# The tail of a fused convolution and SiLU network: the last block's second half, output bank by output bank in another order

## The chip, the cores and the metric

The kernel runs on one core of one Trainium2 chip. The metric is device time in microseconds (us): the median of the runs shown, each of which is one execution of the whole program. The engines are named as in the profile: PE is the matrix engine (PEld its weight loads), DVE the vector engine, ACT the scalar engine, POOL the general-purpose engine, SP the engine that issues most transfers. A `q` behind a name (ACTq, SPq) means the engine's own instruction queue, which also issues its transfers.

## The reference

The reference is a lightweight convolution followed by a two-layer network with SiLU between the layers, without a bias. Cut to what matters:

```python
# x: (8, 4096, 192), weight: (8 heads, 7 taps), softmax over the taps
w   = softmax(weight, axis=-1)
y   = causal depthwise convolution of x, 7 taps, 24 channels per head
h   = y.reshape(32768, 192) @ w_in        # w_in: (192, 2048)
g   = h * sigmoid(h)
out = g @ w_out                           # w_out: (2048, 192)
```

Everything is in float32.

## The kernel before, in words

The 32768 tokens are cut into 32 blocks of 1024 tokens, and a block into two halves of 512 (`TB`). Block 0 is computed by plain matrix products. Blocks 1 to 31 use a fast (Strassen-like) scheme in both layers: fewer products of 2x2 blocks, paid for by sums and differences on DVE, ACT and POOL. The order of the work within a block is written out by hand in `PLAN` (lines 66 to 101): each slot between bars names the products of the first layer (`P..`, `E..`), the evictions and SiLUs (`s..`, `C..`, `g..`) and the differences of the second layer (`t.jk`). `pin` (line 103) holds an instruction behind the instruction that was written before it on the same engine, transfers that this engine issues among them. The transfers themselves are not pinned.

The second layer ("the second half" of a block) gathers its result in six accumulation banks, `accs[b][0..5]`, each of 128 partitions by 512 float32 columns. `out_slot(b, j, i, e)` (line 482) issues the products of bank `i` for one of 4 groups `j` of hidden units and one of two halves `e` of such a group: four products, each of which fills 32 partitions of the bank. Partitions 0 to 95 of banks 0 to 4 hold a product of their own; partitions 96 to 127 hold a third of a further product, whose pieces have to be brought to partitions 0 to 95 before they can be added. Bank 5 holds the last piece of one of these in 4 times 128 columns. So the pieces of banks 0, 1 and 2 make up `y`, those of banks 4, 3 and 5 make up `x_`. With `half` given, a slot covers 256 of the 512 columns (a "token half").

The four outputs of a block are quarters of 96 channels by 512 tokens, `c[0]` to `c[3]` (the fast scheme's C11, C21, C12, C22 in the order that the code uses: index modulo 2 is the token half of the block, index divided by 2 the channel half):

```
c[0] = acc0 + y
c[1] = acc0 + acc2 + acc1 + acc4
c[3] = acc0 + acc2 + acc4 + acc3
c[2] = acc0 + acc2 + acc3 + x_
```

Bank 0 reaches all four quarters, bank 2 three, banks 3 and 4 two, bank 1 one, and each set of pieces one.

In blocks 1 to 30 the second half of a block is overlapped with the convolution for the block after it. The last block (31) has nothing behind it. Its groups `j` = 0 and 1 go through `down` (line 520) as in the others, bank by bank within a group; then `finish` (line 651) issues the groups 2 and 3 in an order of its own. Within it `step(b, "t.jk")` makes the differences for group `j` (line 480, DVE, 128 x 1024; `t.j0`, `t.j1` lie in one tile, `t.j2`, `t.j3` in a second). Bank 0 and bank 1 need no differences, bank 2 needs `t.j1`, bank 4 needs `t.j0` and `t.j3`, bank 3 needs `t.j2` and `t.j3`, bank 5 needs `t.j3`. The tiles of the differences come from `tpool`, which has three buffers.

Before the change `finish` issues, for each of the two groups, banks 2, 4, 3 and 5; then bank 0 for both groups, then bank 1 for both groups, by token halves. Lines 688 to 701 read banks 2, 4, 3 and 5 while PE works on banks 0 and 1. Lines 710 to 715 add bank 0 to the quarters and store `c[3]` and `c[2]`. Lines 716 to 722 add bank 1 and store `c[1]` and `c[0]` by token halves; there POOL makes the sum `c[0] + y` (line 721).

`store` (line 673) transposes a quarter in blocks of 32 x 32 on DVE into `osb` and issues three transfers to memory, the first and third on SP, the second on ACT. All DVE and ACT instructions in `finish` are pinned, the POOL sum and the transfers are not. In the profile all pinned DVE instructions of `finish` carry line 111, the line of the helper.

Of the kernel before, what the change touches and what calls it, by code (L numbers as in the profile page):

```python
# [9 lines left out]
F32 = mybir.dt.float32  # L10
I32 = mybir.dt.int32
AF = mybir.ActivationFunctionType
ALU = mybir.AluOpType
# [4 lines left out]
def kernel(  # L18
# [24 lines left out]
    nc = tc.nc  # L43
# [6 lines left out]
    P = 128  # L50
# [4 lines left out]
    TB = 512  # L55
# [4 lines left out]
    NJ = NM // 2  # L60
    SQ = 32
    HD = D // 2
    NP = HD // SQ
# [6 lines left out]
    xpool = ctx.enter_context(tc.tile_pool(name="xp", bufs=1))  # L70
    tpool = ctx.enter_context(tc.tile_pool(name="tp", bufs=3))
# [31 lines left out]
    def pin(ins):  # L103
        return tc.keep_in_program_order(ins)
# [5 lines left out]
        def __getattr__(self, name):  # L110
            return lambda *args, **kw: pin(getattr(self.engine, name)(*args, **kw))  # L111

    vec = Pinned(nc.vector)

    def bank():
        return psum.tile([P, TB], F32, tag="ps", name="ps")
# [170 lines left out]
    for e in range(2):  # L287
        half = hot[R * e : R * e + R]
# [24 lines left out]
    for k in range(NK):  # L313
# [4 lines left out]
            op=ALU.mult,  # L318
# [96 lines left out]
    bk, us, sums, cmbs, accs = {}, {}, {}, {}, {}  # L415

    def product(b, m, name):
        d, t = dups[b], wins[b]
        e, r, s = m % 2, wr[m // 2], ws[m // 2]

        other, bn, w, v = {
            "P1": (0, "1", r[:, 0, 0, :], d[:, 0, 0, :]),
            "P6": (0, "1", r[:, 0, 1, :], t[:, 1, :]),
            "P7": (0, "1", r[:, 1, 0, :], t[:, 2, :]),
            "P4": (0, "1", r[:, 1, 1, :], t[:, 3, :]),
            "E21": (0, "1", r[:, 1, 2, :], d[:, 0, 2, :]),
            "P2": (1, "b", s[:, 0, 1, :], d[:, 0, 1, :]),
            "E11": (1, "b", s[:, 0, 2, :], d[:, 0, 2, :]),
            "P5": (1, "d", s[:, 1, 0, :], t[:, 0, :]),
            "E22": (1, "d", s[:, 1, 2, :], d[:, 1, 2, :]),  # L430
            "P3": (1, "d", s[:, 0, 0, :], d[:, 1, 1, :]),
            "E12": (1, "d", s[:, 1, 1, :], d[:, 1, 2, :]),
        }[name]
        half = e ^ other
        first = (b, m, bn) not in bk
        if first:
            bk[b, m, bn] = bank()
        pin(
            nc.tensor.matmul(  # L439
                bk[b, m, bn], rows(w, half), rows(v, half), start=first, stop=True,  # L440
                skip_group_check=True,
            )
        )
# [38 lines left out]
    def out_slot(b, j, i, e, half=None):  # L482

        g = [gs[b, j, a] for a in range(2)]
        w, x_ = wo[j], wx[j]
        if i not in accs.setdefault(b, {}):
            accs[b][i] = bank()

        def t(k):
            return sums[b, j][k // 2][:, k % 2, :].rearrange("p (e t) -> p e t", e=2)

        a_ = [[w[:, a, :, HD * u : HD * u + HD] for a in range(2)] for u in range(2)]
        forms = {
            1: lambda: (a_[0][0], g[0][:, 0]),
            2: lambda: (a_[0][1], g[1][:, 0]),
            3: lambda: (x_[:, 2], g[1][:, 1]),
            4: lambda: (a_[1][1], t(3)),
            5: lambda: (x_[:, 0], t(0)),  # L500
            6: lambda: (x_[:, 1], t(1)),
            7: lambda: (a_[1][0], t(2)),
        }
        own, other, c = ((1, 2, 0), (3, 2, 1), (6, 2, 2), (7, 4, 0), (5, 4, 1), (4, 4, 2))[i]
        for q in range(4):
            lhs, rhs = forms[own if q < NP else other]()
            k = c if i == 5 or q == NP else q
            to = slice(0, TB // 4) if i == 5 else slice(0, TB) if half is None else ts(half, TB // 2)
            pin(
                nc.tensor.matmul(  # L510
                    accs[b][i][SQ * q : SQ * q + SQ, to],
                    lhs[:, e, SQ * k : SQ * k + SQ],
                    rhs[:, e, ts(q, TB // 4) if i == 5 else to],
                    start=j == 0 and e == 0,
                    stop=j == NJ - 1 and e == 1,
                    skip_group_check=True,
                )
            )
# [72 lines left out]
    osbs = {}  # L591
# [21 lines left out]
    def step(b, token):  # L613

        if token[0] == "-":
            b, token = b - 1, token[1:]
        name, arg = token.split(".") if "." in token else ("", "")
        if b < 0 or b >= NB or not name or (b, token) in did:
            return
        did.add((b, token))  # L620
        digits = [int(c) for c in arg]
        if name[0] in "PE":
            product(b, digits[0], name)
        elif name[0] in "sCg":
            if b:
                sums_h(b, name, digits[0])
        elif name == "t":
            sum_g(b, *digits)
        elif name[0] in "Mzyx":
            merge(b, name)  # L630
        elif name == "o":
            turn_out(b, *digits)
        elif b + 1 < NB:
            {"i": turn_in, "v": conv, "w": win}[name](b + 1, *digits)
            if name == "v" and digits[1] == K - 1 and (b, "down") in did:
                spread(b + 1, digits[0])
                if digits[0] == NK - 1 and b + 2 < NB:
                    load(b + 2)
# [12 lines left out]
    def finish(b):  # L651


        late = (NJ - 2, NJ - 1)
        for j in late:
            for k in (0, 1, 3, 2):
                step(b, f"t.{j}{k}")
            for i in (2, 4, 3, 5):
                for e in range(2):
                    out_slot(b, j, i, e)  # L660
        acc, n = accs[b], HD
        cmb = xpool.tile([P, 4, TB], F32, tag="cmb", name="cmb")
        cmbs[b] = [cmb]
        c = [cmb[0:n, i, :] for i in range(4)]
        y, x_ = (upool.tile([P, TB], F32, tag="u", name="u") for _ in range(2))

        def part(t, k):
            return t[SQ * k : SQ * k + SQ, :]

        def add(out_, u, v):  # L670
            vec.tensor_tensor(out_, u, v, op=ALU.add)

        def store(i, cols, rows_=slice(0, n)):

            if b not in osbs:
                osbs[b] = tpool.tile([P, 4, TB // SQ, SQ], F32, tag="t", name="osb")
            osb = osbs[b][:, i, :, :].rearrange("p k c -> p (k c)")
            vec.transpose(osb[rows_, cols], cmb[rows_, i, cols])
            ks = slice(cols.start // SQ, cols.stop // SQ)
            for q in range(rows_.start // SQ, rows_.stop // SQ):  # L680
                ch = HD * (i // 2) + SQ * q
                (nc.sync, nc.scalar, nc.sync)[q % 3].dma_start(
                    out=out_v[2 * b + i % 2][:, ks, ch : ch + SQ],
                    in_=osbs[b][SQ * q : SQ * q + SQ, i, ks, :],
                )

        every = slice(0, TB)
        pin(nc.scalar.copy(c[1], acc[2][0:n, :]))
        pin(nc.scalar.copy(part(y, 2), acc[2][n:P, :]))
        pin(nc.scalar.copy(part(x_, 1), acc[4][n:P, :]))  # L690
        add(c[2], c[1], acc[3][0:n, :])
        pin(nc.scalar.copy(part(x_, 0), acc[3][n:P, :]))
        add(c[3], c[2], acc[4][0:n, :])
        add(c[1], c[1], acc[4][0:n, :])
        for q in range(4):
            pin(
                nc.scalar.copy(
                    part(x_, 2)[:, ts(q, TB // 4)], acc[5][SQ * q : SQ * q + SQ, 0 : TB // 4]
                )
            )  # L700
        add(c[2], c[2], x_[0:n, :])
        for j in late:
            for e in range(2):
                out_slot(b, j, 0, e)
        for half in range(2):
            for j in late:
                for e in range(2):
                    out_slot(b, j, 1, e, half)
            if half == 0:
                for k in (3, 2):  # L710
                    add(c[k], c[k], acc[0][0:n, :])
                    store(k, every)
                add(c[1], c[1], acc[0][0:n, :])
                pin(nc.scalar.copy(c[0], acc[0][0:n, :]))
                pin(nc.scalar.copy(part(y, 0), acc[0][n:P, :]))
        for half in range(2):
            cols = slice(half * TB // 2, (half + 1) * TB // 2)
            add(c[1][:, cols], c[1][:, cols], acc[1][0:n, cols])
            pin(nc.scalar.copy(part(y, 1)[:, cols], acc[1][n:P, cols]))
            store(1, cols)  # L720
            nc.gpsimd.tensor_tensor(c[0][:, cols], c[0][:, cols], y[0:n, cols], op=ALU.add)
            store(0, cols)


    for k in range(NK):
# [36 lines left out]
    for b in range(1, NB):  # L762
# [9 lines left out]
        slots = (None for j in range(NJ // 2 if last else NJ) for _ in down(b, j))  # L772
# [34 lines left out]
```

## Time and profile before

| | us |
|---|---|
| median of 4 runs | 2423.1 (2422.9 to 2423.46) |
| profiled execution, device time | 2422.9 |
| its span, first to last instruction | 2421.2 |
| PE busy | 2390.0 (99% of the span) |
| DVE busy | 2077.5 (86%) |
| ACT busy | 982.6 (41%) |
| POOL busy | 64.5 (3%) |
| first product of `finish` (group 2) | at 2393.76 |
| first product of bank 0 in `finish` | at 2404.94 |
| first product of bank 1 in `finish` | at 2408.37 |
| last product ends | at 2412.01 |
| last transpose starts | at 2416.50 |

Times "at" are counted from the start of the span. The device time is 1.7 us longer than the span, which is what lies around the instructions. A row of the timeline gives start, length, engine, line, operation, output and inputs with their shape, the number of instructions taken together, and in brackets how long the engine had been idle and what ended that idle time. Rows of transfers show when they were issued; the time to landing comes from the view of the transfers.

### The profile page before, as it was taken

What the parts mean: (1) busy time and instruction counts of PE and PEld (TensorE: products, weight loads), DVE (VectorE), ACT (ScalarE), POOL (GpSimd) and SP (SyncE); (2) the same over time, 40 slices, a digit from 0 to 9 for tenths busy, and PEclk for the clock granted to TensorE, in tenths of its full rate; (3) what the DMA queues carried; (4) which work ended last, traced back from release to release, by engine and by line L of the source; (5) the groups of instructions that cost most, each with busy time, mean ns of one, the idle gap of its engine ahead of it and who ended that gap; (6) DMA issues with size and microseconds to landing.
All of it is one profiled execution on the core that took longest, in us unless ns stands there. A gap on an engine that the chain in (4) does not pass through costs nothing.

```text
span 2421.2 us, 43109 instructions
## 1 busy us (share of the span) xinstructions
PE 2390.0 (99%) x17776; PEld 956.9 (40%) x17776; DVE 2077.5 (86%) x2831; ACT 982.6 (41%) x1847; POOL 64.5 (3%) x98
## 2 busy tenths in 40 slices
PE   6999999999999999999999999999999999999998
PEld 4444433334333344333444333443334433334433
DVE  8988888898888988888988889888889888898876
ACT  3134533345433355333454334543334533345432
POOL 3300000000000000000000000000000000000000
PEclk9999999999999999999999999999999999999999
DMA  7321222222222212222222222122222222222220
GB/s 152 73 52 32 45 44 54 41 43 40 37 54 49 43 33 39 50 53 40 41 37 43 53 45 46 34 36 53 53 41 39 36 45 54 43 40 41 36 40 14
DMA packets 454085, 111.65 MB, mean 46 GB/s; under 512 B 423936, under 2 KB 429056, under 8 KB 453888
## 3 DMA queue, kind: packets, MB, share of 16 engines
q1 hardware_dynamic: 450064, 106.89, 23.7%
q8 instruction: 139, 2.28, 0.4%
q0 software_dynamic: 480, 1.58, 0.3%
q10 hardware_dynamic: 3344, 0.42, 0.1%
q14 instruction: 58, 0.48, 0.1%
HBM read 31.49 MB, written 25.17 MB: 23 GB/s over the span
## 4 chain that ended last, share of the span: by engine, by line
PE 98%; DVE 1%; DMA 0%; SPq 0%; issue 0%; ACT 0%; ACTq 0%; POOLq 0%; POOL 0%; DVEq 0%
PE ps L439 49%; PE ps L510 46%; PE ps L538 2%; PE ps L403 2%; DVE nat L353 0%; DMA nat<-in_x_dram 0%; SPq L127 0%; DMA raw<-in_moe_w_in_dram 0%; DVE two L111 0%; DVE cmb L111 0%; DVE osb L111 0%; DVE xt L333 0%; DVE nat L350 0%; DVE mh L111 0%; ACT two L201 0%
## 5 line engine op out<-in xcount | busy, mean ns | idle before, releaser
L439 PE MATMUL ps<-dup,ws 64*128 64x512 f32 x2480 | 869.7, 589 | 0.0
L510 PE MATMUL ps<-g,wo 128*32 128x512 f32 x2984 | 662.2, 592 | 0.0
L463 DVE TENSOR_TENSOR g<-u,ps 128x512 f32<-128x512 f32 x744 | 485.2, 679 | 117.7 <-PE ps L439 88.9
L439 PE MATMUL ps<-win,wr 64*128 64x512 f32 x1488 | 568.8, 589 | 0.1
L510 PE MATMUL ps<-t,wo 128*32 128x512 f32 (+1 forms) x4464 | 500.7, 450 | 0.0
L460 ACT ACTIVATE g<-g 128x512 f32<-128x512 f32 x744 | 444.6, 631 | 99.4 <-DVE g L463 99.4
L439 PEld LDWEIGHTS ps<-dup,ws 64*128 64x128 f32 x2480 | 364.1, 187 | 289.0 <-issue 273.4
L510 PE MATMUL ps<-t,wx 128*32 128x512 f32 x2976 | 452.9, 592 | 0.0
L353 DVE SCALAR_TENSOR_TENSOR nat<-xt,taps,nat 128x512 f32<-128x512 f32 x576 | 431.9, 750 | 15.1
L439 PE MATMUL ps<-dup,wr 64*128 64x512 f32 x992 | 419.3, 596 | 0.0
L454 ACT COPY u<-ps 128x512 f32<-128x512 f32 x496 | 277.8, 588 | 228.4 <-PE ps L439 225.5
L577 ACT COPY cmb<-ps 96x512 f32<-96x512 f32 x30 | 17.4, 581 | 805.5 <-PE ps L510 805.5
L480 DVE TENSOR_TENSOR t<-g,t 128x1024 f32<-128x1024 f32 x248 | 303.4, 1223 | 19.1 <-PE ps L510 8.3
L480 DVE TENSOR_TENSOR t<-g 128x1024 f32<-128x1024 f32 x248 | 299.6, 1219 | 22.7 <-PE ps L510 22.7
L439 PEld LDWEIGHTS ps<-win,wr 64*128 64x128 f32 x1488 | 234.3, 187 | 173.7 <-issue 144.5
L510 PEld LDWEIGHTS ps<-t,wo 128*32 128x32 f32 x4464 | 178.3, 110 | 222.6 <-issue 204.9
L439 PE MATMUL ps<-win,ws 64*128 64x512 f32 x496 | 241.9, 589 | 0.0
L510 PE MATMUL ps<-g,wx 128*32 128x512 f32 (+1 forms) x1512 | 234.6, 585 | 0.0
L510 PEld LDWEIGHTS ps<-t,wx 128*32 128x32 f32 x2976 | 121.9, 110 | 277.6 <-issue 268.3
L589 DVE TENSOR_TENSOR cmb<-cmb,ps 96x512 f32<-96x512 f32 x150 | 102.3, 682 | 135.2 <-ACT u L574 133.1
L439 PEld LDWEIGHTS ps<-dup,wr 64*128 64x128 f32 x992 | 160.8, 187 | 126.8 <-issue 111.7
L510 PEld LDWEIGHTS ps<-g,wo 128*32 128x32 f32 x2984 | 169.4, 110 | 98.3 <-issue 98.3
(67 smaller groups left out, 1211.1 us busy)
## 6 DMA issues: line engine op xcount, KB each, us to landing
dup<-nat SPq DMA_DIRECT2D x384, 128.0 KB, 2.3
nat<-in_x_dram SPq DMA_DIRECT2D x382, 64.0 KB, 2.5
out_dram<-osb SPq DMA_DIRECT2D x376, 64.0 KB, 2.0
raw<-in_moe_w_in_dram SPq DMA_DIRECT2D x16, 192.0 KB, 4.9
raw<-in_moe_w_out_dram SPq DMA_DIRECT2D x8, 384.0 KB, 3.6
ws<-wr POOLq DMA_DIRECT2D x8, 192.0 KB, 4.4
xt<-xt SPq DMA_DIRECT2D x31, 4.5 KB, 1.9
tail<-xt SPq DMA_DIRECT2D x24, 4.5 KB, 1.9
```

Source lines behind the costliest of these rows:

```text
L353: nc.vector.scalar_tensor_tensor(out=dst, in0=src, scalar=tap, in1=dst, op0=ALU.mult, op1=ALU.add)
L403: nc.tensor.matmul(hs[a, n, e], rows(wr[j], e)[:, a, k, :], rows(d, e)[:, n, k, :], start=k == 0, stop=k == NK - 1,)
L439: nc.tensor.matmul(bk[b, m, bn], rows(w, half), rows(v, half), start=first, stop=True, skip_group_check=True,)
L454: pin(copy(u, bk[b, m, "1"]))
L460: pin(nc.scalar.activation(g, g, AF.Silu))
L463: pin(nc.vector.tensor_tensor(g, us.pop((b, m, i)), bk[b, m, bn], op=ALU.add))
L480: pin(nc.vector.tensor_tensor(t[i // 2][:, i % 2, :], u, v, op=ALU.subtract))
L510: nc.tensor.matmul(accs[b][i][SQ * q : SQ * q + SQ, to], lhs[:, e, SQ * k : SQ * k + SQ], rhs[:, e, ts(q, TB // 4) if i == 5 else to], sta ...
L538: nc.tensor.matmul(acc[k][R * n : R * n + R, :], wo[j][:, a, e, R * k : R * k + R], gs[b, j, a][:, n, e, :], start=j == 0 and a == 0 and e ...
L577: pin(nc.scalar.copy(c[0], acc[0][0:n, :]))
L589: pin(nc.vector.tensor_tensor(out_, u, v, op=ALU.add))
```

## The change

It rewrites the order of `finish`. All products, sums, transposes and transfers are still there, apart from what follows.

- The order of the banks is 0, 1, 2, 4 with both groups for each, then bank 3 for its first token half, bank 5, and bank 3 for its second token half. The differences `t.j0`, `t.j1` come first, `t.j3` ahead of bank 2, `t.j2` behind the first sum of `c[2]`.
- `c[0]` and `c[1]` are summed and stored whole; `c[3]` and `c[2]` are finished and stored by token halves at the end. Within the loop over halves, the sums and the store of a half stand between the products of bank 3 for this half and those for the next.
- The sum `c[0] + y` moves from POOL to DVE and is one instruction of 512 columns.
- The copies on ACT are pinned as before, through `act`. Five of them (`c[0]`, and the pieces of banks 0, 1, 2 and 4) cover 512 columns, those of bank 3 are by token halves.
- The second tile of differences for group 3 uses the buffer of `win`, and `osb` the buffer of `dup`, both of which the first layer has done with by then, in place of buffers of `tpool`.

```diff
-    vec = Pinned(nc.vector)
+    vec, act = Pinned(nc.vector), Pinned(nc.scalar)
...
-        for j in late:
-            for k in (0, 1, 3, 2):
-                step(b, f"t.{j}{k}")
-            for i in (2, 4, 3, 5):
-                for e in range(2):
-                    out_slot(b, j, i, e)
-        acc, n = accs[b], HD
+        sums[b, NJ - 1] = {1: xpool.tile([P, 2, 2 * TB], F32, tag="win", name="t")}
...
-                osbs[b] = tpool.tile([P, 4, TB // SQ, SQ], F32, tag="t", name="osb")
+                osbs[b] = xpool.tile([P, 4, TB // SQ, SQ], F32, tag="dup", name="osb")
...
-        pin(nc.scalar.copy(c[1], acc[2][0:n, :]))
-        pin(nc.scalar.copy(part(y, 2), acc[2][n:P, :]))
-        pin(nc.scalar.copy(part(x_, 1), acc[4][n:P, :]))
-        add(c[2], c[1], acc[3][0:n, :])
-        pin(nc.scalar.copy(part(x_, 0), acc[3][n:P, :]))
-        add(c[3], c[2], acc[4][0:n, :])
-        add(c[1], c[1], acc[4][0:n, :])
-        for q in range(4):
-            pin(
-                nc.scalar.copy(
-                    part(x_, 2)[:, ts(q, TB // 4)], acc[5][SQ * q : SQ * q + SQ, 0 : TB // 4]
-                )
-            )
-        add(c[2], c[2], x_[0:n, :])
-        for j in late:
-            for e in range(2):
-                out_slot(b, j, 0, e)
-        for half in range(2):
+        def slots(i, half=None):
             for j in late:
                 for e in range(2):
-                    out_slot(b, j, 1, e, half)
-            if half == 0:
-                for k in (3, 2):
-                    add(c[k], c[k], acc[0][0:n, :])
-                    store(k, every)
-                add(c[1], c[1], acc[0][0:n, :])
-                pin(nc.scalar.copy(c[0], acc[0][0:n, :]))
-                pin(nc.scalar.copy(part(y, 0), acc[0][n:P, :]))
+                    out_slot(b, j, i, e, half)
+
+        for j in late:
+            for k in (0, 1):
+                step(b, f"t.{j}{k}")
+        acc = accs[b]
+        slots(0)
+        act.copy(c[0], acc[0][0:n, :])
+        act.copy(part(y, 0), acc[0][n:P, :])
+        slots(1)
+        act.copy(part(y, 1), acc[1][n:P, :])
+        for j in late:
+            step(b, f"t.{j}3")
+        slots(2)
+        act.copy(part(y, 2), acc[2][n:P, :])
+
+        add(c[2], c[0], acc[2][0:n, :])
+        for j in late:
+            step(b, f"t.{j}2")
+        add(c[0], c[0], y[0:n, :])
+        store(0, every)
+        add(c[1], c[2], acc[1][0:n, :])
+        slots(4)
+        act.copy(part(x_, 1), acc[4][n:P, :])
+        add(c[1], c[1], acc[4][0:n, :])
+        store(1, every)
+        add(c[3], c[2], acc[4][0:n, :])
         for half in range(2):
             cols = slice(half * TB // 2, (half + 1) * TB // 2)
-            add(c[1][:, cols], c[1][:, cols], acc[1][0:n, cols])
-            pin(nc.scalar.copy(part(y, 1)[:, cols], acc[1][n:P, cols]))
-            store(1, cols)
-            nc.gpsimd.tensor_tensor(c[0][:, cols], c[0][:, cols], y[0:n, cols], op=ALU.add)
-            store(0, cols)
+            slots(3, half)
+            if half == 0:
+                slots(5)
+            add(c[3][:, cols], c[3][:, cols], acc[3][0:n, cols])
+            store(3, cols)
+            act.copy(part(x_, 0)[:, cols], acc[3][n:P, cols])
+            if half == 0:
+                for q in range(4):
+                    act.copy(
+                        part(x_, 2)[:, ts(q, TB // 4)], acc[5][SQ * q : SQ * q + SQ, 0 : TB // 4]
+                    )
+            add(c[2][:, cols], c[2][:, cols], acc[3][0:n, cols])
+            add(c[2][:, cols], c[2][:, cols], x_[0:n, cols])
+            store(2, cols)
```

The rest of the program, blocks 0 to 30 and the first half of block 31 among it, is the same.

More of the change, by code (lines that the diff above doesn't have):

```diff
@@ L654, in finish @@
         late = (NJ - 2, NJ - 1)
-        for j in late:
-            for k in (0, 1, 3, 2):
-                step(b, f"t.{j}{k}")
-            for i in (2, 4, 3, 5):
-                for e in range(2):
-                    out_slot(b, j, i, e)
-        acc, n = accs[b], HD
+        sums[b, NJ - 1] = {1: xpool.tile([P, 2, 2 * TB], F32, tag="win", name="t")}
         cmb = xpool.tile([P, 4, TB], F32, tag="cmb", name="cmb")
         cmbs[b] = [cmb]
+        n = HD
         c = [cmb[0:n, i, :] for i in range(4)]
         y, x_ = (upool.tile([P, TB], F32, tag="u", name="u") for _ in range(2))
+        every = slice(0, TB)
         def part(t, k):
@@ L671, in add, with store @@
             vec.tensor_tensor(out_, u, v, op=ALU.add)
-        def store(i, cols, rows_=slice(0, n)):
+        def store(i, cols):
             if b not in osbs:
-                osbs[b] = tpool.tile([P, 4, TB // SQ, SQ], F32, tag="t", name="osb")
+                osbs[b] = xpool.tile([P, 4, TB // SQ, SQ], F32, tag="dup", name="osb")
             osb = osbs[b][:, i, :, :].rearrange("p k c -> p (k c)")
-            vec.transpose(osb[rows_, cols], cmb[rows_, i, cols])
+            vec.transpose(osb[0:n, cols], cmb[0:n, i, cols])
             ks = slice(cols.start // SQ, cols.stop // SQ)
-            for q in range(rows_.start // SQ, rows_.stop // SQ):
+            for q in range(NP):
                 ch = HD * (i // 2) + SQ * q
-                (nc.sync, nc.scalar, nc.sync)[q % 3].dma_start(
+                (nc.sync, nc.scalar, nc.sync)[q].dma_start(
                     out=out_v[2 * b + i % 2][:, ks, ch : ch + SQ],
@@ L685, in store @@
                 )
-        every = slice(0, TB)
-        pin(nc.scalar.copy(c[1], acc[2][0:n, :]))
-        pin(nc.scalar.copy(part(y, 2), acc[2][n:P, :]))
-        pin(nc.scalar.copy(part(x_, 1), acc[4][n:P, :]))
-        add(c[2], c[1], acc[3][0:n, :])
-        pin(nc.scalar.copy(part(x_, 0), acc[3][n:P, :]))
-        add(c[3], c[2], acc[4][0:n, :])
-        add(c[1], c[1], acc[4][0:n, :])
-        for q in range(4):
-            pin(
-                nc.scalar.copy(
-                    part(x_, 2)[:, ts(q, TB // 4)], acc[5][SQ * q : SQ * q + SQ, 0 : TB // 4]
-                )
-            )
```

## The prediction

> **What bounds the kernel now.** The page first: its fourth part says that the chain that ended last is PE for 98%, so up to the tail only PE's time counts, and the change leaves that alone. The windows then cut the tail at the last product:
>
> ```profile
> PE 98%; DVE 1%; DMA 0%; SPq 0%; issue 0%; ACT 0%; ACTq 0%; POOLq 0%; POOL 0%; DVEq 0%
> ```
>
> ```profile
> 2397.00:2412.01 15.01, 15.01 (x196) 5.94 (x188) 8.26 (x11) 3.34 (x8) 0.00 (x0) 1.00 0.06 10
> 2412.01:2421.20 9.19, 0.00 (x0) 0.00 (x0) 2.49 (x6) 1.89 (x4) 1.43 (x2) 0.77 0.47 73
> ```
>
> PE is busy without a gap up to 2412.01; then 9.19 us pass without a product, and that is all a new order of sums can win from. Last, the timeline of the tail and the transfers of its last stretch:
>
> ```profile
> 2405.54 0.58 ACT L692 COPY u<-ps 32x512 f32<-32x512 f32 x1 [1.87 <-DVE cmb L111]
> 2412.03 0.58 ACT L714 COPY cmb<-ps 96x512 f32<-96x512 f32 x1 [4.84 <-DVE cmb L111]
> 2414.89 0.38 ACTq L682 DMA_DIRECT2D out_dram<-osb  x1
> 2415.31 0.37 ACT L719 COPY u<-ps 32x256 f32<-32x256 f32 x1 [1.72 <-DVE cmb L111]
> 2416.50 0.44 DVE L111 STREAM_TRANSPOSE osb<-cmb 96x256 f32<-96x256 f32 x1 [0.86 <-POOL cmb L721]
> ...
> 2417.98 0.32 SPq L682 DMA_DIRECT2D out_dram<-osb  x1
> out_dram<-osb SPq DMA_DIRECT2D x1, 32.0 KB, 2.2
> ```
>
> Three things are to be seen. The last store lands at 2420.2 and the program ends 1.0 later. L719's second copy starts 0.05 after ACT's own transfer issue has ended (2415.27): a pinned copy waits behind a store on its queue. And L692 copies partitions 96 to 127 of bank 3, yet waits until the DVE sum that reads partitions 0 to 95 of that bank is done (it began at 2404.82 and takes 0.68); L714 waits in the same way for the last sum on bank 0. So the program keeps two engines off one bank even if they only read, and other partitions of it.
>
> **A rule on this.** The Trainium skill, "PSUM — Partial Sum Buffer", section "PSUM bank collisions raise a hardware error", says that accesses of two engines to one bank must be kept apart where they fall in the same 32 partitions, whatever the columns. This speaks against products for half 1 beside reads of half 0; the trace is stricter still, by whole banks. By the page's finer form the second sum of `c[2]` needn't wait for the ACT copy, PE would resume 0.4 earlier, and the forecast below would be 0.4 lower.
>
> **The change, part by part.** All times are worked out on the profiled execution, which took 2422.9 (span 2421.2 and 1.7 around it), 0.2 below the median of 2423.1.
>
> *Products.* Their number is the same. `finish` starts at 2393.76. Four whole slots take 3.43 (bank 0: 2404.94 to 2408.37), so banks 0, 1, 2 and 4 end at 2397.19, 2400.62, 2404.05 and 2407.48; half 0 of bank 3 (1.73, from 2408.37 to 2410.10) at 2409.21; bank 5 (0.43 for two slots: 2393.76 to 2399.35 less three banks of 1.715) at 2410.07. Moving banks is free as long as the differences are there. `t.20` is already done by 2386.3. `t.30` takes over the buffer that `t.23` got at 2391.84, `t.23` the one that `t.30` got at 2394.1, `t.33` is freed of its wait by the `win` buffer: all done by 2396.8, and needed from 2400.6. The new homes, `win` and `dup`, are free once the first layer's last products are done (2375.8). ACT's copies of `c0` and of the pieces of banks 0 and 1 (0.58 each) run beside the products of banks 1 and 2. Cost 0; were this cover gone, each microsecond would be PE's.
>
> *DVE up to bank 3.* Durations: sum of 512 columns 0.68, difference 1.22, transpose 0.71, sum of 256 columns 0.38 to 0.42, transpose of 256 0.44; 0.04 between dependent ones, minus 0.08 between independent ones. A reader starts 0.25 after the last product's slot (2408.37 to 2408.62).
>
> | what | start to end |
> |---|---|
> | ACT copies bank 2's piece (0.58) | 2404.30–2404.88 |
> | `c2 = c0 + acc2` | 2404.92–2405.60 |
> | `t.22`, `t.32` (PE needs `t.32` at 2408.34) | 2405.52–2407.87 |
> | `c0 += y` | 2407.79–2408.47 |
> | transpose `c0` | 2408.51–2409.22 |
> | `c1 = c2 + acc1` | 2409.14–2409.82 |
> | ACT: issue of `c0`'s store 0.37, then copy of bank 4's piece | 2409.26–2410.26 |
> | `c1 += acc4` (waits for that copy, by bank) | 2410.30–2410.98 |
> | transpose `c1` | 2411.02–2411.73 |
> | `c3 = c2 + acc4` | 2411.65–2412.30 |
> | `c3 += acc3`, half 0 | 2412.34–2412.76 |
> | transpose `c3` half 0 | 2412.80–2413.24 |
> | ACT: issue of its store 0.37, 0.05, copy of bank 3's piece 0.37 | 2413.27–2414.06 |
> | `c2 += acc3`, half 0 | 2414.10–2414.48 |
>
> The first ACT wait holds up DVE by 0.45, as what is queued behind the store on ACT is the copy that DVE needs; before, the same copies came ahead of all stores. Bank 5's copies (1.05), the second sum of `c2` and its transpose follow by 2416.0 and lie beside PE's wait and half 1.
>
> *The added wait.* Before, both halves of bank 1 were written before anything read it. Now the writes of half 1 of bank 3 stand behind three reads of half 0 and, as banks are kept apart, wait for the last of them: PE resumes at 2414.55 instead of 2410.07. It is a wait of 4.45 with nothing queued on PE but these 16 products, and everything left waits for them. No row of before shows a product wait for a read of other columns. Bounds: 0 (a guard by columns), 4.7 (0.05 more for each semaphore step); I take 4.45, as L692 and L714 are the nearest rows and both waited. Half 1 then takes 1.91 (2410.10 to 2412.01): last product at 2416.46, +4.45.
>
> *The clock.* The trace has a PE wait of this size near the start:
>
> ```profile
> 18.47 10.20 PE L403 MATMUL ps<-dup,wr 64*128 64x512 f32 x32 [18.47 <-DMA dup<-nat]
> 32.09 16.43 PE L403 MATMUL ps<-dup,wr 64*128 64x512 f32 x61 [3.42 <-DVE wr L111]
> ```
>
> ```profile
> 27.60:31.06 3.46, 1.07 (x5) 1.00 0.12 28
> 31.06:34.47 3.41, 2.38 (x6) 0.50 0.86 202
> 34.47:37.89 3.42, 3.42 (x10) 0.50 1.04 210
> 37.89:41.30 3.41, 3.41 (x18) 1.00 1.13 200
> ...
> 2416.50:2417.00 0.50, 0.00 (x0) 0.00 (x0) 0.44 (x1) 0.00 (x0) 0.00 (x0) 0.97 0.80 126
> ```
>
> After 2.39 us of idling (28.67 to 31.06) the granted clock fell to 0.50, stayed there for 6.83 although PE worked on from 32.09 (10 products in 3.42 instead of 18), and after the last product it fell 4.96 later (at about 2416.97). Both events lie on a grid of 3.41. A step of that grid with 2.39 idle brought the fall, one with 1.55 idle (2410.15 to 2413.56) did not. For a wait of 4.45 anywhere on it (first step's idle part x, evenly from 0 to 3.41): x above 2.39 (30%) or below 1.04 (30%) puts all of half 1 at half rate, +1.9; x from 1.04 to 2.06 (30%) a part of it, +1.35; 10% nothing. Bounds 0 and 1.9, mean 1.55; I take 1.5.
>
> The Trainium skill, "TensorE: Matmul & The Clock Gate", section "What's actually happening", halves the clock after a whole idle window of about 3.4 us and lifts it after one busy one. The row above agrees on the rate and not on the rest: the step held 30% of work and the clock still fell. By the page's rule only 30% of phases lie right (4.45 − 3.41 over 3.41), the mean would be 0.6, and the forecast 0.9 lower.
>
> *The tail behind the last product.* Before 9.19. After: 0.06, `c3` 0.42, transpose 0.48, ACT issue 0.40 and copy 0.42, `c2` twice 0.42, transpose 0.48, issue 0.03: 3.13. SP's second transfer 0.36 later (the spacing of its issues at 2410.07 and 2410.43), landing 2.2 (other 32 KB ones 1.6), end 1.0: 6.7, −2.5. Bounds −3.1 (landing 1.6) and −2.0 (0.5 of waiting on SP: its queue waited 1.5 in all for earlier transfers in before). What goes is the POOL sums (0.72 twice, which held DVE for 2.31) and SP's crowding: its twelve issues ran from 2410.07 to 2418.29, now they start at 2409.3 and spread to 2420; ACT's six lie in the table and in the 0.40.
>
> **Sum.** +4.45 + 1.5 − 2.5 = +3.45, 2426.35 for the profiled execution, 2426.6 against the median. 0.2% (4.85), about what a measurement of this kernel can tell from no change, isn't reached.
>
> **The rivals.**
> - *PE does not wait.* DVE is then the bound: with half 0 of `c2` transposed at 2415.49 and no wait for products, the last transpose ends at 2418.4 instead of 2416.94; SP follows 0.36 behind instead of 1.04. +0.8: 2423.9. Against: the two bank waits above.
> - *PE waits, the clock holds.* +1.95: 2425.1. For: the end of the trace, 4.96 before a fall. Against: 31.06.
> - *A second wait, on the differences* (the other side). If the tile of `t.22` and `t.23` is guarded as one, bank 4, which reads `t.23`, waits for `t.32`: from 2404.05 to 2407.92, 3.87 more idling. Bank 4's copy, the DVE chain and half 1 then come 1.9 later, with the clock near certain to fall: +5.8, 2428.9, slower. It decides as soon as bank 4 starts later than about 2407. Against: transposes at 2410.66 wrote `osb` while transfers issued at 2410.07 read another slice of it, so tiles are guarded by slice.
> - *Less than thought:* no PE wait, and ACT copies ahead of the stores. DVE gains 0.45 at `c1`, 0.9 and 0.8 in the halves against the first rival: −1.35, 2421.8. Against: the 0.05 behind the issue at 2415.27.
>
> **Chances.** Forecast 0.66, clock holds 0.14, PE does not wait 0.11, second wait 0.05, less 0.04. Slower by over 0.2%: the second wait and 0.05 of the forecast, 0.10. Faster by 4.85 would leave 4.3 behind the last product, of which two sums, a transpose, issue, landing and end take 4.3 without any copy: 0.01. Same 0.89. The range from 2423.6 to 2427.8 takes in the bounds (−3.1 + 4.45 + 0 = +1.35, −2.0 + 4.7 + 1.9 = +4.6) and most of "does not wait"; it leaves out about 0.18.
>
> **What would show it.** Right: a PE gap of about 4.4 before the last 16 products, released by a DVE sum; granted clock 0.50 in them or just behind; `t.22` and `t.32` without a PE gap; no row on POOL. Wrong: no PE gap; a gap ahead of bank 4; ACT copies of `x_` ahead of the store's issue.

## The result, and the profile after

The changed kernel takes 2426.99 us (median of 40 runs, 2426.28 to 2428.07) against 2423.04 for the kernel before (60 runs, 2422.51 to 2423.85): 3.95 us more, a ratio of 1.0016 with a 95% interval of 1.0012 to 1.0021. That lies within 0.2%, but no run of the one overlaps a run of the other. The forecast was 2426.6.

The profiled execution has a span of 2425.6. First the windows of its tail, cut at the last product of bank 5, at the first and at the last of half 1 of bank 3. A row gives the stretch, its length, the busy time of PE, PEld, DVE, ACT and POOL, the granted clock, the share of the transfer engines and their rate:

```profile
2397.00:2410.66 13.66, 13.66 (x168) 5.08 (x160) 4.89 (x7) 2.87 (x5) 0.00 (x0) 1.00 0.02 3
2410.66:2415.03 4.37, 0.00 (x1) 0.00 (x1) 3.24 (x6) 0.86 (x4) 0.00 (x0) 0.75 0.70 98
2415.03:2418.67 3.64, 3.64 (x32) 1.38 (x32) 0.86 (x2) 0.55 (x3) 0.00 (x0) 0.50 0.26 38
2418.67:2425.60 6.93, 0.00 (x0) 0.00 (x0) 2.14 (x5) 0.37 (x1) 0.00 (x0) 0.50 0.20 30
```

All three terms of the forecast can be read here. PE is idle for 4.37 us in the middle of the tail. The clock is 0.75 on the mean of that stretch, because it falls to 0.50 at its half, and half 1 takes 3.64 where the same 16 products (32 rows) took 1.91 before. Behind the last product 6.93 us are left where there were 9.19.

The timeline of the same stretch, PE, DVE and ACT, shows what released what:

```profile
2415.03 3.64 PE L510 MATMUL ps<-t,wo 128*32 128x256 f32 x32 [4.37 <-DVE cmb L111]
...
2405.30 0.69 DVE L111 TENSOR_TENSOR cmb<-cmb,ps 96x512 f32<-96x512 f32 x1 [8.25 <-ACT u L111]
2405.91 2.35 DVE L480 TENSOR_TENSOR t<-g 128x1024 f32<-128x1024 f32 x2
2410.72 0.68 DVE L111 TENSOR_TENSOR cmb<-cmb,ps 96x512 f32<-96x512 f32 x1 [0.55 <-ACT u L111]
2414.56 0.42 DVE L111 TENSOR_TENSOR cmb<-cmb,ps 96x256 f32<-96x256 f32 x1 [0.84 <-ACT u L111]
2418.74 0.42 DVE L111 TENSOR_TENSOR cmb<-cmb,ps 96x256 f32<-96x256 f32 x1 [2.74 <-PE ps L510]
2420.48 0.42 DVE L111 TENSOR_TENSOR cmb<-cmb,ps 96x256 f32<-96x256 f32 x1 [0.85 <-ACT u L111]
...
2412.18 1.94 ACTq L678 DMA_DIRECT2D out_dram<-osb  x2
2414.16 1.46 ACT L111 COPY u<-ps 32x256 f32<-32x256 f32 x5 [3.47 <-DVE osb L111]
```

PE's last 32 rows wait for the DVE sum at 2414.56, which is the second sum of `c2` for half 0: the last of the three reads of bank 3. That sum waits for ACT's copy of the piece, and the copy for a DVE transpose, because ACT's own store issue stands ahead of it. DVE is idle for 8.25 us before bank 2 is done and then has 2.35 of differences to make while everything waits for it.

### The profile page after: what moved, and what is told of

Read it like the earlier page. It is cut to its first block, busy times and chain, and to the rows that moved or that the text cites. A ratio compares the mean times of both kernels' runs of the same rounds, so it can differ in the third digit from the quotient of the medians.

```text
span 2425.6 us, 43104 instructions
## 1 busy us (share of the span) xinstructions
PE 2391.3 (99%) x17776; PEld 946.0 (39%) x17776; DVE 2077.8 (86%) x2833; ACT 981.9 (40%) x1846; POOL 62.2 (3%) x96
## 4 chain that ended last, share of the span: by engine, by line
PE 98%; DVE 1%; DMA 0%; SPq 0%; ACT 0%; issue 0%; ACTq 0%; DVEq 0%
PE ps L439 49%; PE ps L510 46%; PE ps L538 2%; PE ps L403 2%; DVE nat L353 0%; SPq L127 0%; DMA nat<-in_x_dram 0%; DVE cmb L111 0%; DMA raw<-in_moe_w_in_dram 0%; DVE osb L111 0%; DVE two L111 0%; DVE t L480 0%; ACT u L111 0%; DVE xt L333 0%; ACTq L678 0%
## 5 line engine op out<-in xcount | busy, mean ns | idle before, releaser
L510 PE MATMUL ps<-t,wo 128*32 128x128 f32 (+2 forms) x4496 | 502.5, 450 | 4.4 <-DVE cmb L111 4.4
L510 PE MATMUL ps<-g,wx 128*32 128x512 f32 x1488 | 234.5, 592 | 0.0
```

Source lines behind the costliest of these rows:

```text
L510: nc.tensor.matmul(accs[b][i][SQ * q : SQ * q + SQ, to], lhs[:, e, SQ * k : SQ * k + SQ], rhs[:, e, ts(q, TB // 4) if i == 5 else to], sta ...
```

## The experiments

Three readings stood against each other. Theory W is that of the forecast: PE waits for the reads of half 0, and the clock falls in the wait. Rival O says that the order of banks, sums and stores costs by itself, and PE's gap only lies beside it. Rival H says that the clock has no part. The kernel before was measured again beside the runs. Its median was 2423.19 beside four of them (no read between, 36 products, copies, differences) and 2423.06 beside the other four. The changed kernel has 40 runs, each of the others 11. The 95% intervals of the ratios to before reach about 0.0009 (2.1 us) to each side, and only those of the two fillers are clear of 1; the smaller differences rest on medians and on how far the ranges of runs lie apart.

| kernel | median | range | over before |
|---|---|---|---|
| changed | 2426.99 | 2426.28–2428.07 | +3.95 |
| no read between the halves | 2424.51 | 2424.14–2425.07 | +1.32 |
| filler, 36 products | 2428.74 | 2428.45–2429.33 | +5.55 |
| filler, 20 products | 2425.47 | 2425.05–2426.24 | +2.41 |
| copies ahead of stores | 2424.15 | 2423.44–2424.99 | +0.96 |
| differences early | 2424.84 | 2423.58–2426.34 | +1.65 |
| before, with the wait alone | 2424.81 | 2423.07–2425.51 | +1.75 |
| three together, token halves | 2422.76 | 2422.33–2423.16 | −0.30 |
| three together, bank 3 whole | 2421.05 | 2420.87–2421.40 | −2.01 |

### No read between the halves

```diff
-            slots(3, half)
             if half == 0:
+                slots(3, 0)
                 slots(5)
+                slots(3, 1)
```

> All products of bank 3, both token halves, stand ahead of the first read of it; sums, copies and stores keep the order of the changed kernel. Theory W (PE waits for the reads of half 0, 4.4 us, and the clock falls in the wait): no PE gap, granted clock 1.00 up to the last product, the last transpose 2.9 earlier than in the changed kernel because DVE is then the bound: about 2424.1, 1.1 over before. Rival O (the loss is the new order of banks, sums and stores itself, and PE's gap only lies beside it): no PE gap and still 2426.5 to 2427.

Measured 2424.51, 2.48 less than the changed kernel. PE has no gap, and the windows show its last product at 2412.36 with the clock at 1.00:

```profile
2410.60:2412.36 1.76, 1.76 (x36) 0.78 (x24) 1.63 (x3) 0.06 (x1) 0.00 (x0) 1.00 0.73 102
2412.36:2422.70 10.34, 0.00 (x0) 0.00 (x0) 4.50 (x11) 1.76 (x6) 0.00 (x0) 0.63 0.40 58
```

So O falls as the whole of the cause. It keeps a share: without any wait of PE the kernel is still 1.32 over before, and each of its runs is above each run of before beside it (2422.54 to 2423.84). Behind the last product 10.34 pass, more than the 9.19 of before: DVE, which has 4.50 of work left, is the bound then. This is the first rival of the forecast ("PE does not wait", +0.8), 0.5 too low there.

### A filler in the wait, too long and then fitting

```diff
             if half == 0:
                 slots(5)
+                spare = bank()
+                for _ in range(9):      # 5 in the second kernel
+                    for q in range(4):
+                        pin(nc.tensor.matmul(spare[SQ * q : SQ * q + SQ, :], ...))
```

> The changed kernel with 36 further products of 512 columns into a spare bank, read by nothing, between bank 5 and half 1 of bank 3: 3.9 us of PE work inside the 4.4 us wait. Theory W: the wait stays (PE resumes half 1 at the same time), the clock stays at 1.00, half 1 takes 1.9 instead of 3.6: 1.7 less than the changed kernel, about 2425.2. Rival H (the clock is no part of it, the wait alone costs): unchanged, 2427.0, or later by what the filler delays.

> As the first filler, with 20 products in place of 36. Each of those took 0.215, so 36 overran the wait by 3.3; 20 take 4.3 and fit into it. Theory W: half 1 resumes as in the changed kernel, the clock stays at 1.00 through it, 1.7 less than the changed kernel: 2425.3. Rival H (clock no part of it): 2427.0.

The first expectation was missed, by a wrong size: a product of 512 columns costs PE 0.215, so 36 take 7.7 and not 3.9. The 3.9 is the time of 36 rows of the trace, and a float32 product stands there as two rows (36 products, 72 rows). They overran the wait by 3.35 (7.72 less 4.37), and less the 1.73 of the clock this makes +1.6 against the changed kernel, where +1.75 was measured. What the run was for still shows: half 1 took 1.91. The second filler fits. PE's timeline, the first kernel and then the second:

```profile
2410.66 7.91 PE L722 MATMUL ps<-g,wo 128*32 128x512 f32 x72
2418.38 1.91 PE L510 MATMUL ps<-t,wo 128*32 128x256 f32 x32
```

```profile
2410.08 4.47 PE L722 MATMUL ps<-g,wo 128*32 128x512 f32 x40
2414.63 1.93 PE L510 MATMUL ps<-t,wo 128*32 128x256 f32 x32
```

Measured 2425.47 (2425.3 expected), 1.52 less than the changed kernel, by giving PE more work. H falls: the clock costs 1.5 of the 3.95, and the wait has to be priced apart from it.

### The wait alone, put into the kernel before

```diff
-        for half in range(2):
+        for half in range(1):
             for j in late:
                 for e in range(2):
                     out_slot(b, j, 1, e, half)
...
             cols = slice(half * TB // 2, (half + 1) * TB // 2)
+            if half:
+                for j in late:
+                    for e in range(2):
+                        out_slot(b, j, 1, e, half)
             add(c[1][:, cols], c[1][:, cols], acc[1][0:n, cols])
```

> The kernel before, with one part of the change alone: the products for half 1 of its last bank (bank 1) stand behind the sum, the copy and the stores of half 0. Theory W: PE waits for ACT's copy of half 0, 2410.1 to about 2413.7, and its last product ends at 2415.6, or up to 1.8 later where the clock falls; 0.8 to 2.6 over before, about 2425. Rival O (the wait is harmless by itself): no more than 0.4 over before, 2423.6.

Measured 2424.81, as W had it, and over O's limit; nine of the eleven runs lie above every run of before beside them (2422.48 to 2423.52). PE's timeline names what it waits for:

```profile
2414.25 0.42 PE L510 MATMUL ps<-g,wx 128*32 128x256 f32 x3 [3.36 <-ACT u L723]
```

L723 is ACT's copy of 256 columns of bank 1 in partitions 96 to 127. The row's products write the other 256 columns, in partitions 0 to 95. So the program's guard is by bank, for writes against reads too; the forecast had only reads against reads to go by.

### Copies ahead of the stores

```diff
-            store(3, cols)
             act.copy(part(x_, 0)[:, cols], acc[3][n:P, cols])
+            store(3, cols)
```

(and in the same way `slots(4)` with the copy of bank 4's piece ahead of `store(0, every)`)

> The changed kernel with the copies of the pieces of banks 4 and 3 ahead of the stores that stand before them on ACT. Theory W with the copy held behind the store's issue: PE resumes 1.4 earlier (0.5 at the c1 sum, 0.9 at half 0), half 1's copy comes 0.8 earlier, the clock costs on the mean 0.9 instead of 1.5: about 2424.2. Rival S (the order on ACT doesn't matter, as the sums are bound by DVE): within 0.4 of the changed kernel, 2426.6 to 2427.

Measured 2424.15 (2424.2 expected). PE's wait is 3.05 instead of 4.37:

```profile
2413.74 3.56 PE L510 MATMUL ps<-t,wo 128*32 128x256 f32 x32 [3.05 <-DVE cmb L111]
```

Two store issues of 0.37 on ACT had cost PE 1.3: each waits for a transpose, and the copy behind it waits with it. The rest of the gain can't be read as closely: the runs spread from 2423.44 to 2424.99, the profiled one, in which the clock fell, took 2424.95, and it is in part chance that the median meets the expectation.

### Differences early

```diff
         for j in late:
             step(b, f"t.{j}3")
+            step(b, f"t.{j}2")
...
         add(c[2], c[0], acc[2][0:n, :])
-        for j in late:
-            step(b, f"t.{j}2")
```

> The changed kernel with the differences t.22 and t.32 moved to where DVE idles, ahead of bank 2's sums. Theory W: DVE reaches the reads of bank 3 2.0 earlier, PE waits 2.3 instead of 4.4, the clock costs on the mean 0.5 instead of 1.5: about 2424.0. Rival O: DVE's work is moved, not removed, and the end stays at 2426.5 to 2427.

Measured 2424.84, 0.8 above what was expected, though the wait came out as worked out (2.44, expected 2.3). The windows on the clock's grid, this kernel's and then those of the kernel before with the wait alone, whose steps are counted back from its fall at 2419.26:

```profile
2409.92:2413.33 3.41, 0.96 (x32) 0.62 (x28) 2.30 (x6) 1.03 (x4) 0.00 (x0) 1.00 0.58 83
2413.33:2416.75 3.42, 3.25 (x32) 1.31 (x24) 0.84 (x3) 0.36 (x2) 0.00 (x0) 0.50 0.22 32
```

```profile
2409.02:2412.43 3.41, 1.87 (x36) 0.87 (x28) 3.13 (x5) 0.00 (x0) 0.00 (x0) 1.00 0.21 33
2412.43:2415.85 3.42, 1.60 (x32) 0.94 (x32) 1.41 (x4) 1.53 (x3) 0.73 (x1) 1.00 0.75 111
```

In the first kernel a wait of 2.44 fell into one step of the grid, the clock went to 0.50 at its end and half 1 took 3.47. In the second a longer wait of 3.36 was cut by a step's edge into idle parts of 1.54 and 1.82, and the clock held. So the cost depends on how a run's grid lies, which may also make the wide range of these two kernels (2.8 and 2.4 us, against 0.9 in the kernel with no read between). Each run's mean granted clock bears on this. Of the kernel with the differences early, the three runs at 0.999 are the three fastest (2423.58 to 2424.12), and the others, at 0.997 or 0.998, took 2424.14 to 2426.34; of the one with the copies ahead, the four at 0.999 are the four fastest (2423.44 to 2423.76 against 2424.11 to 2424.99). The kernel before with the wait alone doesn't divide like that: its three fastest runs (2423.07 to 2423.89) are at 0.999, but so is the profiled one, in which the clock held, at 2424.81. What made those three faster stays open.

### The three together

Both kernels have the copies ahead of the stores, the differences early, and no read of bank 3 between its products. The first keeps the token halves of the changed kernel, and with them the order of all its products. The second issues bank 3 whole and bank 5 last:

```diff
-        for half in range(2):
...
+        slots(3)
+        slots(5)
+        act.copy(part(x_, 0), acc[3][n:P, :])
+        add(c[3], c[3], acc[3][0:n, :])
+        for q in range(4):
+            act.copy(part(x_, 2)[:, ts(q, TB // 4)], acc[5][SQ * q : SQ * q + SQ, 0 : TB // 4])
+        add(c[2], c[2], acc[3][0:n, :])
+        store(3, every)
+        for half in range(2):
+            cols = slice(half * TB // 2, (half + 1) * TB // 2)
+            add(c[2][:, cols], c[2][:, cols], x_[0:n, cols])
             store(2, cols)
```

> Like the version with all three, but bank 3 in token halves with bank 5 between, and sums, copies and stores of c3 and c2 by token halves as in the changed kernel. Theory W: no PE gap; four sums more of 256 columns and two transposes more behind the last product than there: the last transpose 4.7 behind the last product, 2422.6. Rival O: 2424 or more.

> The changed kernel with three things undone or moved: bank 3 written whole and then bank 5, before any sum reads bank 3; the copies ahead of the stores on ACT; the differences t.22 and t.32 where DVE idles. The sums of c3 and the first of c2 become whole, the last one and its store stay in token halves. Theory W: no PE gap, no fall of the clock before the last product, the last transpose ends 3.4 behind the last product instead of 4.9 in the kernel before, the last transfer 0.7 behind it: about 2421.2, faster than before by 2. Rival O (the order of banks and stores is what costs): 2424 or more.

Measured 2422.76 and 2421.05; 2422.6 and 2421.2 were expected. The first has no PE gap, and the clock holds:

```profile
2408.78:2412.43 3.65, 3.64 (x84) 2.30 (x76) 1.96 (x3) 0.02 (x1) 0.00 (x0) 1.00 0.59 83
```

It differs from the kernel with no read between by the two moves alone, and they took 1.75 off: the 1.32 that was left there came from the place of the copies and of the differences, and not from the order of the banks, which is still that of the changed kernel. Against before, its 0.30 less is no clear gain, as the ranges overlap. The second beats both kernels: every one of its runs lies below every run of before (ratio 0.9992, interval 0.9983 to 1.0001, so by that interval just not clear of 1). The second kernel's windows, behind the last product:

```profile
2412.13:2415.41 3.28, 0.00 (x1) 0.00 (x0) 3.21 (x7) 1.02 (x4) 0.00 (x0) 1.00 0.27 40
2415.41:2419.40 3.99, 0.00 (x0) 0.00 (x0) 0.00 (x0) 0.00 (x0) 0.00 (x0) 0.61 0.55 78
```

DVE is busy for 3.21 of the 3.28 up to the last transpose, and 3.99 pass with the last transfers and the end of the program.

## Why the prediction was right

*Products.* Right. No gap up to 2410.66, so the differences were in time and the new buffers cost nothing; the rival of a second wait ahead of bank 4 didn't occur.

*DVE up to bank 3.* Right to 0.1. Bank 2's copy starts at 2404.69 instead of the 2404.30 worked out, 0.39 later, and the second sum of `c2` at 2414.56 instead of 2414.10, 0.46 later. The 0.39 lies ahead of `finish`, whose first product starts at 2394.14 instead of 2393.76, in code that isn't changed; single executions of before differ by more (1.34).

*The added wait.* Right, and it was the term with the least ground: 4.37 from the modelled end of the last product, about 4.55 from where the next would have started (an estimate from the forecast's 2410.07 and the 0.39), 4.45 forecast. The kernel before with the wait alone shows the guard itself. It is not the finer guard by 32 partitions that the prediction weighed.

*The clock.* The mechanism was right, the size a little low: 1.73 in the profiled run (3.64 less 1.91) and 1.52 between medians, 1.5 taken. (The 10 and 18 products that the prediction counts at the start are rows, two to a product; the rates stand.) What failed is the chance behind it. A step with 2.39 us idle was the lowest that had shown a fall, so 10% of phases were given as safe and 30% as partly so. In the changed kernel's profile a step of 3.41 with 1.25 of work, 2.16 idle, brought it:

```profile
2409.41:2412.82 3.41, 1.25 (x40) 0.89 (x32) 2.73 (x5) 0.58 (x1) 0.00 (x0) 1.00 0.41 58
2412.82:2416.23 3.41, 1.20 (x12) 0.59 (x16) 2.14 (x5) 1.39 (x5) 0.00 (x0) 0.50 0.60 87
```

The start of the profile with 36 filler products goes lower: there (PE alone) a step with 1.43 of work, 1.98 idle, brought it too.

```profile
27.15:30.56 3.41, 1.43 (x7) 1.00 0.00 0
30.56:33.98 3.42, 1.54 (x4) 0.50 0.74 161
```

With the 1.82 that did not, the edge lies between 1.82 and 1.98 in these profiles, and a wait of 4.4 can't miss it: split in two, one part is always over 2.1. The rule of the Trainium skill, "TensorE: Matmul & The Clock Gate", section "What's actually happening", that it takes a whole idle window of 3.4 us, does not hold here: the clock fell in waits of 2.44 and 3.05. On the clock's rise after one busy window the rule fares better than the prediction said: the step that did not lift the clock at the start was busy for 2.38 of 3.41, and with 3.35 busy in the kernel with the copies ahead the clock was back one step later:

```profile
2413.68:2417.09 3.41, 3.35 (x32) 1.39 (x32) 0.87 (x3) 1.02 (x4) 0.00 (x0) 0.50 0.54 78
2417.09:2420.50 3.41, 0.21 (x4) 0.00 (x0) 2.10 (x5) 0.37 (x1) 0.00 (x0) 1.00 0.21 30
```

*The tail.* 6.93 instead of 9.19, −2.26 where −2.5 was taken. The last transpose begins at 2421.38, 2.71 behind the last product, where the sum makes 2.62. The rest of the missing 0.2 lies behind it: the last transfer of SP was issued at 2422.52, 0.70 behind the end of that transpose and not 0.39, and landed in 2.0 instead of 2.2.

*The sum.* 4.55 + 1.73 − 2.26 = +4.02 for the profiled execution, and 0.39 from ahead of `finish`: 4.4, which is the difference of the spans (2425.6 and 2421.2). The medians differ by 3.95, the forecast was +3.45.

One reading of the sum would go too far. Its terms are right on the path as it was, but they aren't what each undoing gives back: without the wait and the clock the kernel gained 2.48, not 6.3, since DVE's chain then ends last. Undone one after the other, the clock gives back 1.5 (filler), the wait 1.0 more (no read between the halves), and 1.3 are left for the order of work on DVE and ACT, which the two moves took away.

## What to carry to other kernels

A bank cut into halves so that sums can start early helps only if nothing of it is read before all of it is written: here products of other columns of the same bank waited for every read in front of them. Price a PE wait twice, as idle time and as half-rate work behind it, and see whether spare work in the wait is cheaper than the fall. Before reordering a tail, look for work that can go into idle time ahead of it (the differences), and for transfer issues that stand in front of copies on the same queue; with both moved and no read between the halves, the new bank order cost nothing (0.30 less than before, within the spread), and with bank 3 whole and bank 5 behind it the kernel was 2.0 faster.

## What the runs showed of the hardware

The clock fell at the end of steps of a 3.41 us grid, which lay differently in every profile (falls in the tail at 2412.82, 2413.33 and 2413.68). The steps can be read off the falls and rises: 2413.68 and 2417.09 are one step apart, 31.06 and 37.89 in the kernel before are two. It fell where PE had been idle for 1.98 us or more of a step, and not with 1.82 or less. So a wait of 3.36 left the clock at 1.00, though it cost its own time, and one of 2.44 made the 16 products behind it take 3.47 instead of 1.91. Adding 20 products that nothing reads made a kernel 1.5 us faster.
